# Loading the weights of a two-layer expert network in pairs of pieces: one transfer of 1 MB in place of two of 512 KB

## Chip, cores and metric

One core of one Trainium2 chip. The metric is device time in microseconds (us) of the whole kernel, the median of its runs. In the profile PE is TensorE (matmuls; PEld are its weight loads), DVE VectorE, ACT ScalarE, POOL GpSimd, SP SyncE, whose queue (SPq) issues nearly all transfers here. Lnnn is a line of the kernel.

## The reference, cut to what matters

Chunked attention (4 batches, 8 heads, 768 positions of 64), then a soft mixture of 8 experts with 4 slots each, then a dense layer with a softmax-like activation, layer normalisation and an output matrix:

```python
# attention, per chunk of 32 queries: 8 memory keys + up to 56 keys around it
scores = scale * np.matmul(q_c, k_full.transpose(0, 1, 3, 2))
out[:, :, c_start:c_end] = np.matmul(softmax(scores), v_full)
# experts: x is [3072, 512], phi [512, 32], w1 [8, 512, 1024], w2 [8, 1024, 512]
slot_input = softmax_over_tokens(x @ phi).T @ x
for e in range(E):
    h = np.maximum(slot_input[e] @ w1[e], 0.0)
    slot_out[e] = h @ w2[e]
x = softmax_over_slots(x @ phi) @ slot_out
# dense: w_in [512, 1024], w_out [1024, 512]
h = x @ w_in
solu = h * softmax(h)
return (layer_norm(solu) * g_ln) @ w_out
```

All is float32. The weights w1 and w2 are 33.6 MB, w_in and w_out 4.2 MB, the packed keys, queries and values 25.9 MB.

## The kernel before, in words

**Attention** (lines 841 to 874) runs over 32 groups g, each half a sequence of one pair of heads. Every engine has its order written out by hand. In group g, PE multiplies queries and keys of group g + 1 (`emit_qk`, L254), then the weights and values of group g - 1 (`emit_pv`, L310), and turns blocks round for groups g and g - 3 (L292, L321). SP issues the packed keys and queries of group g + 4 (`load_qk`, 400 KB, L188, into 4 buffers in turn), then `load_e(LOADS[g])`, weight pieces ahead of their use, then the values of group g + 3 in two transfers (`load_v`, L202, 4 buffers; it waits for the `emit_pv` that read the buffer). `emit_spread` (L299 to L303) moves the keys of group g + 3 to the layout that PE reads: those with an odd number on POOL alone, those with an even number on ACT and POOL. PE's product for a group waits for its spread. A few groups carry more work: logits and running sums of the experts' slots, and from group 3 on the casts of w_in to a wider form (`win_ops`; floats on ACT, L577, others on DVE and POOL), which give the raw piece's slot back.

**Weight pieces.** All weights come as 80 pieces of 512 KB, [128 partitions, 1024 floats], rows of 4096 bytes. The list `chunks` fixes their order: w_in and w_out in turn (8 of w_in, 7 of w_out), then the experts' units, two pieces to a unit, then the last piece of w_out. A unit is half of an expert's w1 or w2; there are 32, in the order w1(0,0), w1(0,1), w1(1,0), w2(0,0), w1(1,1), w2(0,1), w1(2,0), and so on to w2(7,0), w2(7,1). `load_e(n)` (lines 219 to 236) issues the next n pieces of the list, and stops at the first that finds no free slot. w_out has slots of its own (w0 to w7). All else takes the first of the list `free`: 4 pieces in e1, 9 in e2, 4 in e3, and the slot w7 that the last piece of w_out needs only at the end. The slots of e3 and w7 are used by expert weights once (`once`). `release` gives a slot back after its last reader. As attention ends, its buffers become slots as well (`more`): 5 in a0 from group 30 on, then 1 in x2, 6 in a1, 1 in x0. A transfer into such a slot waits for the last reader of what lay there.

**Experts** (lines 931 to 951): for each unit n, `emit_w1` (L497) or `emit_w2` (L515), 4 matmul steps, each on half a piece; a turn of w1's result (L504), with work of ACT and DVE between; then `release` of the unit's two pieces and `load_e()`. Steps of the casts of w_out and of the tokens' weights run beside them.

**Dense layer** (from line 953): on PE 24 tiles of 24 matmuls (L723), which with their surroundings take the second half of the kernel. Its weights are in SBUF by then.

The loads in attention are set by one list, and the pieces issued by the end of group g are g - 1 from group 5 on:

```python
LOADS = [0] + [1, 1, 1, 0] + [1] * 28
```

Of the kernel before, what the change touches and what calls it, by code (L numbers as in the profile page):

```python
# [16 lines left out]
P = 128  # L17
# [12 lines left out]
DM = H * D  # L30
KC = DM // P
E, SE, FF = 8, 4, 1024
NSLOT = E * SE
FC = FF // P
# [7 lines left out]
NE = 25  # L42
CAST0, CASTN, NEARLY = 3, 3.4, 8
VLEAD = 3
LOADS = [0] + [1, 1, 1, 0] + [1] * 28
LANE, SIDE = 2.6, 1

CASTU = (0, 1, 2, 3, 4, 5, 6)
# [31 lines left out]
def tile_kernel(ctx: ExitStack, tc: tile.TileContext, kr, vr, w1, w2, w_in, w_out, cst, out):  # L80
    nc = tc.nc
    pe, dve, act, pool, sp = nc.tensor, nc.vector, nc.scalar, nc.gpsimd, nc.sync
# [76 lines left out]
    w_in_f = at("win", 0, KC * FF)  # L159
    w_in_sb = w_in_f.rearrange("p (k f) -> p k f", k=KC)  # L160
    mhi = at("win", 0, FF, FP32R)
    free = [at(n, 1024 * i, 1024) for n, c in (("e1", 4), ("e2", 9), ("e3", NE - 13 - FC)) for i in range(c)]
    wslot = [at(f"w{j}", 0, 1024) for j in range(FC)]
    once = free[13:]
    free.append(wslot[-1])
    whi, wlo = {}, {}

    sint = at("misc", 0, 128).rearrange("p (k s) -> p k s", k=KC)
# [36 lines left out]
    for e in range(E - 1):  # L205
        units += [("w1", e + 1, 0), ("w2", e, 0), ("w1", e + 1, 1), ("w2", e, 1)]
    units += [("w2", E - 1, 0), ("w2", E - 1, 1)]
    chunks = [(w, j) for j in range(2 * KC) for w in ("win", "wout")][:-1]
    for u in units:
        chunks += [u[:2] + (2 * u[2] + j,) for j in range(2)]  # L210
    chunks.append(("wout", FC - 1))
    slot_of = {}
    nxt = [0]

    def more(name, n):

        free.extend(at(name, 1024 * i, 1024) for i in range(n))

    def load_e(n=99):
        while n and nxt[0] < len(chunks):  # L220
            key = chunks[nxt[0]]
            if key[0] == "wout":
                slot = wslot[key[1]]
            elif free:
                slot = free.pop(0)
            else:
                break
            slot_of[key] = slot
            if key[0] in ("w1", "w2"):
                src = (w1 if key[0] == "w1" else w2)[key[1], key[2]]  # L230
                sp.dma_start(out=slot.rearrange("p (k f) -> p k f", k=2), in_=src)
            else:
                src = (w_in if key[0] == "win" else w_out)[key[1]]
                sp.dma_start(out=slot.bitcast(I64), in_=src)
            nxt[0] += 1
            n -= 1

    def release(key):
        if slot_of[key] is wslot[-1]:
            return  # L240
        if key[0] == "win" or not any(slot_of[key] is x for x in once):
            free.append(slot_of[key])


    def kwin(i, c):
# [751 lines left out]
def layout(inputs):  # L997
    import numpy as np

    q, k, v = inputs["q"], inputs["k"], inputs["v"]  # L1000
    mk, mv = inputs["mem_k"], inputs["mem_v"]
    f = np.float32
    a = {}
    qv = q.reshape(B, PAIRS, 2, 2, GTOK, D).transpose(0, 3, 1, 2, 5, 4)
    fill = mk[:, :, 0:1, :]
    kp = np.concatenate([np.repeat(fill, 16, 2), k, np.repeat(fill, NREC * CH - S - 16, 2)], 2)
    kp = np.stack([np.concatenate([kp[:, :, CH * i:CH * (i + GREC) - NMEM], mk], 2) for i in (0, GCH)], 1)
    kp = kp.reshape(B, 2, PAIRS, 2, KT, D).transpose(0, 1, 2, 3, 5, 4)
    a["kr"] = np.concatenate([kp, qv], -1).reshape(GROUPS, P, KT + GTOK)
    vp = np.zeros((B, H, NREC * CH, VW), f)  # L1010
    vp[:, :, 16:16 + S, 0:D] = v
    vp[:, :, 16:16 + S, D] = 1.0
    vp = vp.reshape(B, H, NREC, CH, VW)
    mp = np.ones((B, H, NCH, NMEM, VW), f)
    mp[..., 0:D] = mv[:, :, None]
    vp = np.concatenate([vp[:, :, 0:NCH], mp, vp[:, :, 1:NREC, 0:WIN - REC]], 3)
    vp = vp.reshape(B, PAIRS, 2, 2, GCH, WIN, VW).transpose(0, 3, 1, 2, 5, 4, 6)
    a["vr"] = np.ascontiguousarray(vp).reshape(GROUPS, 2, WIN, VS)
    a["w1"] = np.ascontiguousarray(
        inputs["moe_w1"].reshape(E, 2, 2, P, 2, 512).transpose(0, 4, 1, 3, 2, 5).reshape(E, 4, P, 2, 512)  # L1020
    )
    a["w2"] = np.ascontiguousarray(inputs["moe_w2"].reshape(E, 4, 2, P, DM).transpose(0, 1, 3, 2, 4))
    a["w_in"] = np.ascontiguousarray(
        inputs["moe2_w_in"].reshape(DM, FC, 4, 32).transpose(0, 2, 1, 3).reshape(KC, P, 2, 512).transpose(0, 2, 1, 3).reshape(2 * KC, P, 512)
    ).view(np.int64)
# [33 lines left out]
```

## Time and profile before

| | us |
|---|---|
| three runs, median (lowest to highest) | 333.23 (332.99 to 333.95) |
| the profiled execution, its own time | 334.36 |
| its span, first to last instruction | 332.5 |
| PE busy in the span | 300.8 (90%) |
| DVE, ACT, POOL busy | 239.4, 223.1, 169.9 |
| moved by the DMA engines | 95.86 MB |

The span is cut into 40 equal slices of 8.3 us; a digit is the busy share in tenths, GB/s what the 16 DMA engines moved. An issue's duration is the time that SP's queue is occupied with it; its landing is counted from the start of the issue. A wait is put down to what ended it.

### The profile page before, as it was taken

The numbers are of one execution on the slowest core, as the hardware profiler recorded it, in microseconds if no ns is written. First come the engines' busy times: TensorE is split into PE (matmuls) and PEld (weight loads), VectorE is DVE, ScalarE is ACT, GpSimd is POOL, SyncE is SP. The second block draws the span as 40 slices with busy tenths as digits, with TensorE's granted clock in tenths as the row PEclk, the third lists the DMA queues.
The fourth block names the chain that finished last, engine by engine and source line by source line (L and its number), as shares of the span: only waits on it lengthen the run. The fifth ranks groups of instructions, "written<-read, shape, count | busy, mean of one in ns | idle before, by whom it ended". The sixth has DMA issues, their size and how long they took to land.

```text
span 332.5 us, 8398 instructions
## 1 busy us (share of the span) xinstructions
PE 300.8 (90%) x3069; PEld 218.1 (66%) x3069; DVE 239.4 (72%) x432; ACT 223.1 (67%) x441; POOL 169.9 (51%) x398
## 2 busy tenths in 40 slices
PE   2979698897897789888999999999999999999996
PEld 2667576675675533332434788888888888888885
DVE  6686887797768438999117886897888778787540
ACT  3476656764765427685524779998888888888721
POOL 5436567566767023222100357777767677676600
PEclk9999999999999999999999999999999999999999
DMA  7999999999999999999950004667666756666531
GB/s 286 366 359 405 407 399 411 412 411 414 409 407 396 418 417 419 415 421 416 417 228 0 0 34 158 252 206 264 207 244 211 246 209 201 240 231 234 202 95 64
DMA packets 39433, 95.86 MB, mean 288 GB/s; under 512 B 4832, under 2 KB 15456, under 8 KB 39392
## 3 DMA queue, kind: packets, MB, share of 16 engines
q1 hardware_dynamic: 39248, 95.11, 75.3%
q8 instruction: 24, 0.39, 0.5%
q10 hardware_dynamic: 144, 0.22, 0.2%
q14 instruction: 17, 0.14, 0.1%
HBM read 78.53 MB, written 16.78 MB: 287 GB/s over the span
## 4 chain that ended last, share of the span: by engine, by line
PE 56%; DMA 32%; DVE 5%; ACT 2%; issue 2%; POOL 1%; SPq 1%; ACTq 0%; POOLq 0%
PE bank L723 37%; DMA kq_area<-in_kr_dram 19%; DMA ex_area<-in_w_dram 6%; DMA e_area<-in_w_dram 6%; PE h L635 4%; PE bank L254 3%; PE bank L310 2%; PE bank L497 1%; POOL kq_area L303 1%; PE bank L292 1%; DMA vz_area<-in_vr_dram 1%; PE bank L515 1%; PE bank L733 1%; PE t L733 1%; PE t L692 1%
## 5 line engine op out<-in xcount | busy, mean ns | idle before, releaser
L723 PE MATMUL bank<-wh_area,yh_area 128*128 128x512 f32 x552 | 129.8, 390 | 0.0
L723 PEld LDWEIGHTS bank<-wh_area,yh_area 128*128 128x128 f32 x552 | 103.4, 188 | 21.8
L303 POOL TENSOR_SCALAR kq_area<-kq_area 64x416 f32<-64x416 f32 x88 | 38.5, 443 | 38.5 <-DMA kq_area<-in_kr_dram 27.9
L254 PE MATMUL bank<-kq_area 128*32 128x128 f32 x768 | 29.8, 293 | 16.8 <-POOL kq_area L303 10.8
L706 DVE STREAM_TRANSPOSE yq_area<-yq_area 128x1024 f32<-128x1024 f32 x20 | 24.9, 1246 | 17.2 <-DMA yq_area<-z 17.2
L254 PEld LDWEIGHTS bank<-kq_area 128*32 128x32 f32 x768 | 21.0, 116 | 23.1 <-POOL kq_area L303 15.2
L650 DVE SCALAR_TENSOR_TENSOR eb_area<-h,eb_area 128x1024 f32<-128x1024 f32 x24 | 29.0, 1213 | 9.2 <-ACT eb_area L644 9.0
L295 ACT COPY s_area<-bank 128x384 f32<-128x384 f32 x32 | 15.2, 476 | 27.7 <-PE bank L292 26.1
L310 PE MATMUL bank<-vz_area,s_area 128*32 128x130 f32 x768 | 29.7, 279 | 2.2 <-ACT s_area L295 1.6
L272 DVE TENSOR_REDUCE cst_area<-bank 128x6 f32<-128x384 f32 x32 | 17.7, 554 | 19.2 <-PE bank L254 19.0
L688 POOL TENSOR_SCALAR cst_area<-cst_area 128x1 f32<-128x1 f32 x72 | 26.6, 369 | 7.6
L641 DVE TENSOR_REDUCE cst_area<-h 128x1 f32<-128x1024 f32 x24 | 29.0, 1216 | 0.9 <-PE h L635 0.9
L644 ACT ACTIVATE eb_area<-h,cst_area 128x1024 f32<-128x1024 f32 x24 | 26.6, 1110 | 1.9 <-DVE cst_area L641 1.9
L673 ACT ACTIVATE eb_area<-eb_area,cst_area 128x1024 f32<-128x1024 f32 x24 | 27.3, 1138 | 0.1
L677 POOL TENSOR_SCALAR cst_area<-cst_area 128x1 f32<-128x1 f32 x24 | 15.9, 662 | 21.7 <-ACT eb_area L644 19.8
L717 DVE TENSOR_TENSOR yh_area<-yq_area,yh_area 128x1024 fp32r<-128x1024 f32 x20 | 24.5, 1224 | 2.3 <-ACT yh_area L713 2.3
L670 ACT ACTIVATE eb_area<-eb_area,cst_area 128x1024 f32<-128x1024 f32 x20 | 23.1, 1155 | 4.3 <-DVE eb_area L650 3.8
L310 PEld LDWEIGHTS bank<-vz_area,s_area 128*32 128x32 f32 x768 | 22.3, 111 | 5.0 <-ACT s_area L295 2.8
L689 POOL TENSOR_SCALAR cst_area<-cst_area 128x1 f32<-128x1 f32 x72 | 21.9, 304 | 7.1
L713 ACT CAST yh_area<-yq_area 128x1024 fp32r<-128x1024 f32 x20 | 21.0, 1049 | 6.3 <-DVE yq_area L706 6.3
L741 ACT ACTIVATE eb_area<-bank,cst_area 128x512 f32<-128x512 f32 x23 | 15.8, 685 | 8.8 <-POOL cst_area L679 5.9
L299 ACT COPY kq_area<-kq_area 64x416 f32<-64x416 f32 (+1 forms) x34 | 12.2, 407 | 11.2 <-DMA kq_area<-in_kr_dram 11.1
(154 smaller groups left out, 534.2 us busy)
## 6 DMA issues: line engine op xcount, KB each, us to landing
e_area<-in_w_dram SPq DMA_DIRECT2D x37, 512.0 KB, 8.5
ex_area<-in_w_dram SPq DMA_DIRECT2D x26, 512.0 KB, 10.0
kq_area<-in_kr_dram SPq DMA_DIRECT2D x32, 400.0 KB, 6.3
vz_area<-in_vr_dram SPq DMA_DIRECT2D x64, 195.0 KB, 6.3
z<-eb_area SPq DMA_DIRECT2D x20, 512.0 KB, 2.7
yq_area<-z SPq DMA_DIRECT2D x80, 128.0 KB, 2.9
out_dram<-eb_area SPq DMA_DIRECT2D x23, 256.0 KB, 2.1
e_area<-in_w_in_dram SPq DMA_DIRECT2D x8, 512.0 KB, 6.4
```

The lines of the kernel that those rows point to most:

```text
L254: pe.matmul(out=bk[32 * j:32 * j + 32, t * 128:(t + 1) * 128], lhsT=kq[i][:, KT + c * CH:KT + (c + 1) * CH], rhs=kwin(g % 2, c), start=Tru ...
L303: pool.tensor_scalar(out=o, in0=i, scalar1=1.0, scalar2=0.0, op0=ALU.mult, op1=ALU.add)
L310: pe.matmul(out=bk[32 * j:32 * j + 32, t * 2 * VW:(t + 1) * 2 * VW], lhsT=atb[g % 2][:, c * CH:(c + 1) * CH], rhs=vz[g % 4][:, :, c * VW:( ...
L641: dve.tensor_reduce(out=sc("nm", i), in_=fin["h"][i % 2], axis=AX.X, op=ALU.max, negate=True)
L644: act.activation(out=eb[i % FIN], in_=fin["h"][i % 2], func=ACTF.Exp, bias=sc("nm", i), accum_out=sc("s", i))
L650: dve.scalar_tensor_tensor(out=ub[i % FIN], in0=fin["h"][i % 2], scalar=-1.0 / FF, in1=eb[i % FIN], op0=ALU.mult, op1=ALU.mult, accum_out= ...
L670: act.activation(out=yb[i % FIN], in_=ub[i % FIN], func=ACTF.Identity, scale=-float(FF), bias=sc("nu", i))
L673: act.activation(out=sq, in_=ub[i % FIN], func=ACTF.Square, scale=-float(FF), bias=sc("nu", i), accum_out=sc("vs", i))
L688: pool.tensor_scalar(out=t, in0=r, scalar1=r, scalar2=xx, op0=ALU.mult, op1=ALU.mult)
L706: dve.transpose(out=yv[i % FIN].rearrange("p (f a t) -> p a f t", f=FC, a=4), in_=yq[i % FIN].rearrange("p (a f t) -> p a f t", f=FC, a=4),)
L717: dve.tensor_tensor(out=yl[i % FIN][:, sl], in0=tps(i, sl) if i < NPE else yv[i % FIN], in1=yh[i % FIN][:, sl].bitcast(FP32), op=ALU.subtract,
L723: pe.matmul(out=fin["o"][i % 2], lhsT=a[i % FIN][:, f * 128:(f + 1) * 128], rhs=w[f], start=start, stop=stop)
```

## The change

The two pieces of a unit, and pieces 2j and 2j + 1 of w_in, become one transfer of 1 MB with rows of 8192 bytes into a pair of neighbouring slots. Pieces of w_out, the first unit and the last two units stay single. Slots are split in two lists: `free` has the pairs (2 in e1, 4 in e2, 2 in e3, later 2 in a0 and 3 in a1), `ones` the odd pieces (the ninth of e2, w7, later one each in a0, x2, x0). A pair is given back when both its pieces are. The order of the list becomes: a pair of w_in, two single pieces of w_out, and so on; then the units as before. A call of `load_e` counts pieces and may go one over. The list LOADS now has two pieces in every second group; the host lays the weights out so that a pair's row is contiguous. The code that reads the weights is the same.

```diff
-LOADS = [0] + [1, 1, 1, 0] + [1] * 28
+LOADS = [0, 2, 0, 2, 0] + [0, 2] * 14
...
-    free = [at(n, 1024 * i, 1024) for n, c in (("e1", 4), ("e2", 9), ("e3", NE - 13 - FC)) for i in range(c)]
+    free = [at(n, 2048 * i, 2048) for n, c in (("e1", 2), ("e2", 4), ("e3", (NE - 13 - FC) // 2)) for i in range(c)]
     wslot = [at(f"w{j}", 0, 1024) for j in range(FC)]
-    once = free[13:]
-    free.append(wslot[-1])
+    once = free[6:]
+    ones = [at("e2", 8 * 1024, 1024), wslot[-1]]
...
+    def halves(u):
+        return [u[:2] + (2 * u[2] + j,) for j in range(2)]
+
+    chunks = []
+    for j in range(0, 2 * KC, 2):
+        chunks.append([("win", j), ("win", j + 1)])
+        chunks += [[("wout", i)] for i in (j, j + 1) if i < FC - 1]
+    for n, u in enumerate(units):
+        chunks += [[x] for x in halves(u)] if n == 0 or n >= len(units) - 2 else [halves(u)]
+    chunks.append([("wout", FC - 1)])
...
-        free.extend(at(name, 1024 * i, 1024) for i in range(n))
+        free.extend(at(name, 2048 * i, 2048) for i in range(n // 2))
+        if n % 2:
+            ones.append(at(name, 1024 * (n - 1), 1024))
...
-        while n and nxt[0] < len(chunks):
-            key = chunks[nxt[0]]
+        while n > 0 and nxt[0] < len(chunks):
+            keys = chunks[nxt[0]]
+            kind, two = keys[0][0], len(keys) == 2
...
+            elif free if two else ones:
+                slot = (free if two else ones).pop(0)
             else:
                 break
...
-            n -= 1
+            n -= len(keys)
...
     def release(key):
-        if slot_of[key] is wslot[-1]:
+        slot, keys, two, kind = pair_of[key]
+        gone.add(key)
+        if not all(k in gone for k in keys) or slot is wslot[-1]:
             return
-        if key[0] == "win" or not any(slot_of[key] is x for x in once):
-            free.append(slot_of[key])
+        if kind == "win" or not any(slot is x for x in once):
+            (free if two else ones).append(slot)
...
-        inputs["moe_w1"].reshape(E, 2, 2, P, 2, 512).transpose(0, 4, 1, 3, 2, 5).reshape(E, 4, P, 2, 512)
+        inputs["moe_w1"].reshape(E, 4, P, 2, 512).transpose(0, 3, 2, 1, 4)
```

## Rows read from the trace of the kernel before

**Rows 1.** The page: the DMA engines in 40 slices of 8.3 us.

```profile
DMA  7999999999999999999950004667666756666531
GB/s 286 366 359 405 407 399 411 412 411 414 409 407 396 418 417 419 415 421 416 417 228 0 0 34 158 252 206 264 207 244 211 246 209 201 240 231 234 202 95 64
```

**Rows 2.** Stretches: us, busy of PE, PEld, DVE, ACT, POOL, clock, DMA share, GB/s.

```profile
14.00:21.00 7.00, 7.00 (x174) 5.68 (x165) 5.35 (x15) 4.89 (x13) 2.40 (x6) 1.00 0.93 307
60.00:95.00 35.00, 30.68 (x669) 23.98 (x669) 27.84 (x73) 24.28 (x68) 21.30 (x39) 1.00 1.03 411
124.00:136.00 12.00, 11.64 (x95) 4.41 (x91) 10.06 (x24) 9.09 (x21) 3.40 (x4) 1.00 1.03 420
```

**Rows 3.** Timeline of SP's queue, 9 to 15 us, and of ACT at 20.

```profile
9.63 0.43 SPq L234 DMA_DIRECT2D e_area<-in_w_in_dram  x1
12.88 1.12 SPq L202 DMA_DIRECT2D vz_area<-in_vr_dram  x2
...
14.67 0.94 SPq L234 DMA_DIRECT2D w_area<-in_w_out_dram  x1
...
19.98 0.69 ACT L577 ACTIVATE cst_area<-e_area 128x512 f32<-128x512 f32 x1
```

**Rows 4.** The last keys: issue and landing (min/median/max), then POOL's and PE's timeline.

```profile
L188 SPq DMA_DIRECT2D kq_area<-in_kr_dram x1: 333/333/333, 94.9 to 94.9; - x1
...
DMA to landing us min/median/max: 6.3/6.3/6.3
...
101.36 2.12 POOL L303 TENSOR_SCALAR kq_area<-kq_area 64x416 f32<-64x416 f32 x4 [0.23 <-DMA kq_area<-in_kr_dram]
...
103.54 0.86 PE L254 MATMUL bank<-kq_area 128*32 128x128 f32 x24 [1.37 <-POOL kq_area L303]
```

**Rows 5.** DMA queues: packets, MB, share of 16 engines; 128.5 to 131.5, 38.0 to 38.4 us.

```profile
q1 hardware_dynamic: 344, 1.26, 102.4%
...
q14 instruction: 1, 0.01, 4.8%
```

**Rows 6.** Timeline of SP's queue around the first units, from 119 us.

```profile
119.87 0.33 SPq L231 DMA_DIRECT2D ex_area<-in_w_dram  x1
123.40 7.78 SPq L231 DMA_DIRECT2D e_area<-in_w_dram  x8
...
124.30 0.38 SPq L231 DMA_DIRECT2D e_area<-in_w_dram  x1
...
129.91 0.33 SPq L231 DMA_DIRECT2D e_area<-in_w_dram  x1
```

**Rows 7.** The 43rd piece of weights: issue, and time to landing.

```profile
L231 SPq DMA_DIRECT2D ex_area<-in_w_dram x1: 328/328/328, 116.1 to 116.1; - x1
...
DMA to landing us min/median/max: 10.1/10.1/10.1
```

**Rows 8.** Timeline of PE: the first two units of the experts, and the last two.

```profile
122.31 1.92 PE L497 MATMUL bank<-e_area,cst_area 128*32 128x512 f32 x16 [0.27 <-DVE cst_area L426]
...
168.04 1.97 PE L515 MATMUL bank<-e_area,hr_area 128*32 128x512 f32 x8
170.24 2.21 PE L515 MATMUL bank<-e_area,hr_area 128*32 128x512 f32 x8 [0.24 <-DMA e_area<-in_w_dram]
```

**Rows 9.** The chain that ended last, 125 to 175 us: start, us, what.

```profile
161.61 9.74 DMA e_area<-in_w_dram
...
171.40 1.05 PE bank L515 x4
```

**Rows 10.** Issues by line, KB each, median us to landing; last, the keys' min/median/max.

```profile
z<-eb_area SPq DMA_DIRECT2D x20, 512.0 KB, 2.7
yq_area<-z SPq DMA_DIRECT2D x80, 128.0 KB, 2.9
e_area<-in_w_in_dram SPq DMA_DIRECT2D x8, 512.0 KB, 6.4
...
DMA to landing us min/median/max: 4.0/6.3/7.3
```

More of the change, by code (lines that the diff above doesn't have):

```diff
@@ L207, in tile_kernel @@
     units += [("w2", E - 1, 0), ("w2", E - 1, 1)]
[L208 to L212, printed above, removed]
+    def halves(u):
[4 more added lines that the diff above has]
+        chunks += [[("wout", i)] for i in (j, j + 1) if i < FC - 1]
@@ L213, in tile_kernel @@
+    for n, u in enumerate(units):
+        chunks += [[x] for x in halves(u)] if n == 0 or n >= len(units) - 2 else [halves(u)]
+    chunks.append([("wout", FC - 1)])
+    slot_of, pair_of = {}, {}
     nxt = [0]
     def more(name, n):
-        free.extend(at(name, 1024 * i, 1024) for i in range(n))
+        free.extend(at(name, 2048 * i, 2048) for i in range(n // 2))
+        if n % 2:
+            ones.append(at(name, 1024 * (n - 1), 1024))
     def load_e(n=99):
-        while n and nxt[0] < len(chunks):
-            key = chunks[nxt[0]]
[L222 to L225, printed above, removed]
+        while n > 0 and nxt[0] < len(chunks):
+            keys = chunks[nxt[0]]
+            kind, two = keys[0][0], len(keys) == 2
+            if kind == "wout":
+                slot = wslot[keys[0][1]]
+            elif free if two else ones:
+                slot = (free if two else ones).pop(0)
@@ L226, in load_e @@
             else:
                 break
[L228 to L231, printed above, removed]
+            for i, key in enumerate(keys):
+                slot_of[key] = slot[:, 1024 * i:1024 * i + 1024]
+                pair_of[key] = (slot, list(keys), two, kind)
+            if kind in ("w1", "w2"):
+                src = (w1 if kind == "w1" else w2)[keys[0][1], keys[0][2] // 2]
+                if not two:
+                    half = keys[0][2] % 2
+                    src = src[:, 2 * half:2 * half + 2]
+                sp.dma_start(out=slot.rearrange("p (k f) -> p k f", f=512), in_=src)
@@ L232, in load_e @@
             else:
-                src = (w_in if key[0] == "win" else w_out)[key[1]]
+                src = w_in[keys[0][1] // 2] if kind == "win" else w_out[keys[0][1]]
                 sp.dma_start(out=slot.bitcast(I64), in_=src)
             nxt[0] += 1
-            n -= 1
+            n -= len(keys)
+    gone = set()
     def release(key):
-        if slot_of[key] is wslot[-1]:
+        slot, keys, two, kind = pair_of[key]
+        gone.add(key)
+        if not all(k in gone for k in keys) or slot is wslot[-1]:
@@ L1019, in layout @@
     a["w1"] = np.ascontiguousarray(
-        inputs["moe_w1"].reshape(E, 2, 2, P, 2, 512).transpose(0, 4, 1, 3, 2, 5).reshape(E, 4, P, 2, 512)
+        inputs["moe_w1"].reshape(E, 4, P, 2, 512).transpose(0, 3, 2, 1, 4)
     )
-    a["w2"] = np.ascontiguousarray(inputs["moe_w2"].reshape(E, 4, 2, P, DM).transpose(0, 1, 3, 2, 4))
+    a["w2"] = np.ascontiguousarray(inputs["moe_w2"].reshape(E, 2, 4, P, DM).transpose(0, 1, 3, 2, 4))
     a["w_in"] = np.ascontiguousarray(
-        inputs["moe2_w_in"].reshape(DM, FC, 4, 32).transpose(0, 2, 1, 3).reshape(KC, P, 2, 512).transpose(0, 2, 1, 3).reshape(2 * KC, P, 512)
+        inputs["moe2_w_in"].reshape(DM, FC, 4, 32).transpose(0, 2, 1, 3).reshape(KC, P, 1024)
     ).view(np.int64)
```

## The prediction

> **What bounds the kernel now.** I read the slices of the page first. The DMA engines are busy to the full from the second slice to the twentieth, that is from 8 to 166 us, at 359 to 421 GB/s, and then stop [rows 1]. The weights, the queries, keys and values all pass in that time, so the first half of the kernel is a stream of bytes. The stages say the same with more detail: from 60 to 95 us the stream runs at 411 GB/s with PE at 30.7 of 35 us, from 124 to 136 us at 420 GB/s; only from 14 to 21 us is there a shortfall, 307 GB/s at a busy share of 0.93, while PE is full [rows 2]. At its other end, the last weight piece of 512 KB is issued at 161.61 us, lands 9.74 us later, and 1.05 us of matmuls behind it end the expert stage at 172.45 [rows 9]. Those 9.74 us are 7.8 pieces at 420 GB/s (1.25 us each): SP keeps eight transfers in the air, in order. What follows 172.45 is fixed work on PE with weights that are already there. So the question is when that last piece lands, and when PE could be done without it.
>
> PE's side of it: its last two units stretch to 1.97 and 2.21 us, where the first two took 1.92 together [rows 8]. Without the DMA they would end at about 168.04 + 1.92 = 170.0 us, 2.4 us before the real end. More than that a faster stream cannot give, unless the expert stage starts earlier.
>
> **The change part by part.**
>
> *Fewer, longer transfers.* 4 pairs of w_in and 29 of the 32 units' pairs become one transfer each: 33 issues less, at 0.33 us of SP [rows 6]. SP waits in this stage, for landings and free slots, so this alone is worth nothing. The bytes are the same. A row of 4096 bytes costs 102.4% of 16 x 3.0 us over 1.26 MB, 307 rows of 4096 bytes (the other 37 packets only tell of an end), or 160 ns; a packet of 8192 bytes that stands alone in its queue, one of instructions, takes 4.8% of 16 x 0.4 us, 307 ns [rows 5]. Two rows against one: 13 ns at most, call it 11 without the end packets; over the 8 rows that each of the 16 engines has of a pair that is 0.09 us a pair, 2.9 us for 33. Nothing at all is the other end, if the packet starts that it saves lie under their neighbours (the share is over 100%). I take the middle, 0.044 us a pair, b = 1.45 us in all, because that packet belongs to another kind of transfer.
>
> The Trainium skill ("DMA: Bandwidth & Descriptors", Where 436 GB/s comes from) puts the ports' limit at 435 GB/s; by it 34.6 MB would gain at most 2.9 us over 420 GB/s (an estimate), and the sum below would be 0.3 us where it is 1.35.
>
> *The early order.* In group 1 the kernel now queues two pieces instead of one (issue at 9.63 us), and none in group 2 (14.67) [rows 3]; groups 3 and 4 have two and none. SP then stands until 12.88 for PE, and behind this comes the shortfall: 2.15 MB in 7.0 us would take 5.23 us at 411 GB/s, so 1.77 us are lost [rows 2]. A piece more in the queue is 1.25 us of work just ahead of the hole. I take a = 1.25 us gained; bounds 0 (if the shortfall only moves) and 1.8 (all of it). Nothing new is waited for there: such a piece lands 6.4 us after its issue [rows 10], the pair then at about 9.63 + 6.4 + 1.25 = 17.3, and the first cast runs on ACT at 19.98 [rows 3].
>
> *The order of weights against keys.* Counting the pieces that load_e has issued through group 26: 25 before (LOADS is 1 a group from group 5 on), 27 after, since group 18 takes a half and a whole pair, three pieces for its 2. The last keys, kq(31), are issued at 94.90 in group 27 behind these, and land 6.3 us later at 101.2; POOL spreads them from 101.36, and PE, idle for 1.37 us, starts on them at 103.54 [rows 4]. They are what the end of the attention waits for. Two pieces more ahead of them cost 2.5 us; of these the early order takes off 1.25, and the 9 pairs that are through by then 0.40. PE's expert stage starts x = 0.85 us later: 122.31 [rows 8] becomes 123.16. By itself this is covered, for the stage then has 2.4 us to spare against the DMA; with that cover gone it costs 0.85.
>
> *Slots.* The region arithmetic decides the rest. Before, 46 pieces fit ahead of the first unit's matmuls; after, 13 pair slots and 5 single ones hold fewer in order, since three singles (the odd ends of the regions that come free late) can only take the last two units: 43 pieces are issued, and the 44th, half of unit 14's pair, waits until unit 1 gives its pair back (the first unit returns a single, which no pair can use). Before, the SP queue shows the same wait without damage: it issues the 46th piece at 119.87, waits for PE until 123.40, and has 6 us of work in the air. After, this cover is gone. The 43rd piece was issued at 116.1 and landed 10.1 us later, 126.2 [rows 7]; with 1.25 and 17 pairs x 0.044 off that is 124.2. The pair's release came at 124.30 (the issue behind unit 1's wait) [rows 6], after the change at 125.15. So the queue is empty, and a fresh transfer needs its own delay L before bytes arrive. L from rows: a 512 KB store lands in 2.7 us, less 1.25 of bytes, 1.45; a 128 KB fetch in 2.9, less 0.31, 2.6; the first keys of the program in 4.0, less 0.98, 3.0 [rows 10]. I take 2.4, near the fetch, which reads HBM as this does, and on the short side because the core is not cold. The hole is S1 = 125.15 + 2.4 - 124.2 = 3.35 us.
>
> A second one follows. Units 3 and 4 lie in slots that are used once, so unit 16's pair waits for unit 5, whose release let SP issue at 129.91 [rows 6]; that becomes 130.76, and bytes come at 133.16. Units 14 and 15 have landed by 125.15 + 2.4 + 2 x 2.46 = 132.47. S2 = 0.7 us. From unit 6 on a slot comes back with each unit, faster than the 2.46 us that a pair needs, and the stream holds.
>
> **The sum.** The last piece lands at 171.35 - 1.25 (a) - 1.45 (b) + 3.35 + 0.7 = 172.7. PE, from 170.0 + 0.85 = 170.85, is ready before, so the DMA still sets the end, 1.35 us later than now. Written out with the unknowns left in: 1.3 + L - a - 0.75 b (what delays or hurries the keys moves the dry moment and the release alike). The profiled execution took 334.36 us, 332.5 of it span, and is 1.13 above the median of the three runs; I put the 1.35 on that median: 333.23 + 1.35 = 334.6 us.
>
> **The rivals.**
>
> *The stream never runs dry, and the change is a gain.* If the transfers in the air still cover 125 to 128 us, S1 and S2 are nothing, the last piece lands at 168.7, and PE sets the end at 170.85, 1.6 us before the present one: 331.6 us. It decides at one point, whether unit 14's pair is issued at least L before unit 13's has landed. For it: before, there were 6.5 us in hand there (119.87 + 10.1 against 123.40) [rows 6, 7], and my count takes 3 pieces, 3.75 us, and 2.5 us from these. Against it: that leaves nothing for L, whose smallest row is 1.45. A page's rule leads the same way: the Trainium skill ("DMA: Bandwidth & Descriptors", Rules for kernel authors) wants at least 1 MiB per transfer for full bandwidth. The trace differs on pieces of 512 KB, which already run at 420 GB/s [rows 2] with eight in the air. 0.15.
>
> *It cancels.* a and b near their upper ends and L near its lowest: 1.3 + 1.45 - 1.8 - 0.75 x 2.0 = -0.5; with L at 1.8, about -0.2. Taken as no change, 333.2 us. 0.27.
>
> *Rows of 8192 bytes are cut.* If the queue makes two packets of 4096 of each, b is 0 and the sum is 1.3 + 2.4 - 1.25 = 2.5: 335.7 us. Only the packet size of another queue speaks against it [rows 5]. The Trainium skill ("DMA: Bandwidth & Descriptors", SWDGE vs HWDGE vs iDMA) prefers packets of at most 4096 bytes, which would be this case; no weight row before is longer, so no run here shows it. 0.08.
>
> *The attention limps.* Keys with an odd number now come 4.4 us behind the even ones instead of 3.2, the even ones 2.0 behind these. Two groups take 6.4 us of stream and 2 x 3.2 x 30.7 / 35 = 5.6 of PE [rows 2], so the waits ought to merge; if 0.2 us were lost in each of 13 rounds, unit 1's release would come 2.6 us later still, the hole would grow by it, and the time be 337.2. 0.05.
>
> **How the numbers follow.** 0.45 is left for the forecast, 334.6, with its own range of 333.6 to 336.5. A measurement of this kernel can tell 0.3%, 1.0 us, from no change. Of the forecast's 0.45 a part of 0.10 falls below 334.2 and counts as the same. Slower: 0.35 + 0.08 + 0.05 = 0.48; same: 0.27 + 0.10 = 0.37; faster: 0.15. The range takes in the cancelling case and the gain, which is its lower end, and above it L at 3.0 with nothing of a: 1.3 + 3.0 - 1.1 = 3.2, 336.5.
>
> **What would show it.** In the slices the GB/s should dip once, in the slice or two between 124 and 133 us, and 14 to 21 us should fill up. SP's wait in line with the release of unit 1 should end at about 125, with the landing of unit 13's pair ahead of it, and the transfer behind it should land within 5 us instead of 16 or more. The last keys should land at about 102, the last piece near 172.7, with PE waiting for it. 8192-byte rows should show as half the packets. I am wrong if the stream stays full through 124 to 133 us (the slots were miscounted), if the keys land earlier than 101 (the order costs nothing), or if the last piece lands before 171 with the hole in place (a longer row saves more than I allow).

## The result, and the profile after the change

| | us |
|---|---|
| before, median of 6 runs (lowest to highest) | 333.68 (332.99 to 334.63) |
| after, median of 6 runs | 337.55 (336.34 to 341.1) |
| ratio, 95% interval | 1.0126 [1.0076, 1.0175] |
| after, the profiled execution and its span | 336.34, 334.5 |
| forecast, its range | 334.6, 331.6 to 336.5 |

The change makes the kernel slower, as forecast, but by 3.9 us where 1.4 was said, and outside the range. The profiled execution is the fastest of the six, so what it shows is the mildest case. A ratio leaves out the runs more than 1.5% above the fastest of the same kernel, which the medians and spans beside it take in: two in all, 341.49 us in *No triple load* and 336.55 us in the second run of *Both edits*.

First the page of after, DMA engines in 40 slices (against [rows 1]), and its packets on the main queue.

```profile
DMA  7999999999999979999960004656666665766521
GB/s 291 388 407 387 411 412 415 412 419 413 408 415 399 402 288 361 421 428 423 413 272 0 1 33 157 240 207 251 228 238 206 231 222 179 264 222 236 208 89 64
...
q1 hardware_dynamic: 34496, 95.11, 73.8%
```

The early slices are fuller than before, and there is one dip that was not there, slices 15 and 16, from 117 to 134 us. Before, the same queue had 39248 packets for the same 95.11 MB: 4752 less, which is 33 transfers x 128 rows and 16 end packets for each. So rows of 8192 bytes go as one packet.

The stretches of [rows 2], after (us, busy of PE, PEld, DVE, ACT, POOL, clock, DMA share, GB/s):

```profile
14.00:21.00 7.00, 5.65 (x118) 4.24 (x122) 4.71 (x13) 3.42 (x10) 2.40 (x6) 1.00 1.02 403
60.00:95.00 35.00, 27.44 (x629) 21.97 (x622) 24.91 (x66) 22.14 (x64) 21.45 (x38) 1.00 1.03 413
124.00:136.00 12.00, 11.65 (x99) 4.46 (x99) 10.14 (x24) 9.09 (x21) 3.48 (x4) 1.00 0.90 337
```

The shortfall of 14 to 21 us is filled, 403 GB/s for 307; but PE, full there before, now works 5.65 of the 7 us, and 27.44 of the 35 from 60 us, where it had 30.68. The hole is in the last row, 337 GB/s for 420.

The hole from near by: the timeline of SP's queue from 112 to 134 us, what SP waited for there, then the two transfers at its edge, unit 13's pair (issue, time to landing) and unit 14's.

```profile
112.12 1.28 SPq L245 DMA_DIRECT2D ex_area<-in_w_dram  x3
124.24 9.25 SPq L245 DMA_DIRECT2D e_area<-in_w_dram  x6
...
SPq L245 <- PE bank L515: 12.9, 4, 10.8
...
L245 SPq DMA_DIRECT2D ex_area<-in_w_dram x1: 432/432/432, 113.0 to 113.0; - x1
...
DMA to landing us min/median/max: 11.6/11.6/11.6
...
L245 SPq DMA_DIRECT2D e_area<-in_w_dram x1: 327/327/327, 124.2 to 124.2; - x1
...
DMA to landing us min/median/max: 4.7/4.7/4.7
```

SP has three pairs out by 113.4 us and then stands 10.8 us for PE, until unit 1 gives its pair back at 124.24. Unit 13's pair lands at 113.0 + 11.6 = 124.6, so the queue is empty as the next one is issued. That one lands 4.7 us later, at 128.91, and so 4.31 us behind its forerunner, where a pair in a full stream needs 2.45: 1.9 us more. It does not end there. By the trace the next pairs land at 132.07, 134.54, 137.70, 140.76 and 143.20: three of these steps take 3.1 us instead of 2.45, 2.0 us more.

The bytes tell where the loss lies. First one line of before, then four of after:

```profile
112.00:124.00 12.00, 9.91 (x85) 4.92 (x80) 4.29 (x15) 3.75 (x15) 2.14 (x2) 1.00 1.03 418
```

```profile
112.00:124.00 12.00, 9.91 (x84) 4.91 (x80) 4.29 (x15) 3.78 (x16) 2.15 (x2) 1.00 0.88 358
124.00:128.90 4.90, 4.90 (x44) 1.99 (x44) 3.18 (x9) 4.56 (x11) 0.51 (x1) 1.00 0.75 244
128.90:132.00 3.10, 3.10 (x28) 0.97 (x24) 3.00 (x8) 1.63 (x5) 1.72 (x2) 1.00 0.99 373
132.00:143.00 11.00, 9.58 (x79) 3.28 (x71) 10.56 (x23) 7.75 (x19) 2.13 (x3) 1.00 1.01 422
```

Against 418 GB/s, 1.7 us are missing already before 124, while the last pairs of the queue land, 2.0 to 128.9 and 0.4 to 132: 4.1 us in all. From 132 us on the stream is full, so the late landings at 137.70 and 140.76 are no new holes; they show at the landings what was lost before.

The last keys (issue, landing, POOL's spread, PE's product, against [rows 4]), PE's longest wait in the attention, its first unit, and the end of the chain:

```profile
L188 SPq DMA_DIRECT2D kq_area<-in_kr_dram x1: 535/535/535, 94.5 to 94.5; - x1
...
DMA to landing us min/median/max: 7.1/7.1/7.1
...
101.74 1.88 POOL L321 TENSOR_SCALAR kq_area<-kq_area 64x416 f32<-64x416 f32 x4 [0.54 <-PE bank L328]
...
103.67 0.86 PE L272 MATMUL bank<-kq_area 128*32 128x128 f32 x24 [1.30 <-POOL kq_area L321]
...
77.62 0.86 PE L272 MATMUL bank<-kq_area 128*32 128x128 f32 x24 [3.33 <-POOL kq_area L321]
...
122.25 0.62 PE L515 MATMUL bank<-e_area,cst_area 128*32 128x512 f32 x2 [0.27 <-DVE cst_area L444]
...
158.10 15.20 DMA e_area<-in_w_dram
173.30 0.04 issue
173.35 1.05 PE bank L533 x4
```

The last keys land at 101.6, and the experts begin at 122.25, as early as before. The last piece lands at 173.30, 1.94 us later than in the profile of before, and the time is 1.98 longer: half of the 3.9 us between the medians. The other half is that after's profile lies 1.2 us below its median and before's 0.7 above. The wait of 3.33 us before 77.62 is new: before, PE's longest wait for keys behind the first was 1.82 us. It stands ahead of group 23, whose keys are issued behind the three pieces of group 18.

One identity holds through all that follows. In each of the 17 profiled executions, before and after included, the time less the landing of the last expert piece is 162.9 to 163.15 us. So that landing sets the end, whatever the kernel, and every experiment can be read by it.

A slip of the description ahead: w_in and w_out are stored as float64 (4.2 MB each) and cast to float32 on the chip; no step rests on it.

### The profile page after: what moved, and what is told of

Same layout as the page of the kernel before. It is cut to its first block, busy times and chain, and to the rows that moved or that the text cites. A ratio compares the mean times of both kernels' runs of the same rounds, so it can differ in the third digit from the quotient of the medians.

```text
span 334.5 us, 8330 instructions
## 1 busy us (share of the span) xinstructions
PE 297.9 (89%) x3069; PEld 216.4 (65%) x3069; DVE 236.6 (71%) x432; ACT 222.8 (67%) x441; POOL 170.7 (51%) x398
## 3 DMA queue, kind: packets, MB, share of 16 engines
q1 hardware_dynamic: 34496, 95.11, 73.8%
## 4 chain that ended last, share of the span: by engine, by line
PE 54%; DMA 28%; DVE 10%; ACT 3%; POOL 2%; issue 2%; SPq 0%; ACTq 0%; DVEq 0%; POOLq 0%
PE bank L741 36%; DMA e_area<-in_w_dram 9%; DMA kq_area<-in_kr_dram 7%; DMA w_area<-in_w_out_dram 6%; DMA e_area<-in_w_in_dram 5%; PE h L653 4%; PE bank L272 2%; POOL kq_area L321 2%; PE bank L328 2%; DMA vz_area<-in_vr_dram 1%; PE bank L515 1%; PE bank L351 1%; PE bank L398 1%; PE bank L310 1%; PE bank L751 1%
## 5 line engine op out<-in xcount | busy, mean ns | idle before, releaser
L706 POOL TENSOR_SCALAR cst_area<-cst_area 128x1 f32<-128x1 f32 x72 | 26.8, 372 | 7.6
L328 PE MATMUL bank<-vz_area,s_area 128*32 128x130 f32 x768 | 27.5, 273 | 1.0 <-ACT s_area L313 1.0
L695 POOL TENSOR_SCALAR cst_area<-cst_area 128x1 f32<-128x1 f32 x24 | 15.7, 656 | 23.7 <-ACT eb_area L662 21.8
L691 ACT ACTIVATE eb_area<-eb_area,cst_area 128x1024 f32<-128x1024 f32 x24 | 27.3, 1139 | 0.1
L707 POOL TENSOR_SCALAR cst_area<-cst_area 128x1 f32<-128x1 f32 x72 | 23.4, 324 | 7.1
L328 PEld LDWEIGHTS bank<-vz_area,s_area 128*32 128x32 f32 x768 | 21.4, 108 | 2.2 <-ACT s_area L313 1.9
L305 ACT ACTIVATE s_area<-s_area 128x384 f32<-128x384 f32 x32 | 16.9, 529 | 3.7 <-DVE s_area L296 3.7
```

Source lines behind the costliest of these rows:

```text
L328: pe.matmul(out=bk[32 * j:32 * j + 32, t * 2 * VW:(t + 1) * 2 * VW], lhsT=atb[g % 2][:, c * CH:(c + 1) * CH], rhs=vz[g % 4][:, :, c * VW:( ...
L691: act.activation(out=sq, in_=ub[i % FIN], func=ACTF.Square, scale=-float(FF), bias=sc("nu", i), accum_out=sc("vs", i))
L706: pool.tensor_scalar(out=t, in0=r, scalar1=r, scalar2=xx, op0=ALU.mult, op1=ALU.mult)
L707: pool.tensor_scalar(out=r, in0=t, scalar1=1.5, scalar2=r, op0=ALU.add, op1=ALU.mult)
```

## The experiments

Each was timed in five rounds beside the kernel before, whose medians in the four sets were 333.83, 333.16, 333.08 and 332.94 us. "Clock" is the mean granted clock of a run.

**The changed kernel, again.** No edit.

> The changed kernel once more, for its spread and its granted clock. Slots theory (the DMA queue runs dry between 124 and 131 us, all else is as before): every run within 0.3% of 336.3 us, clock 1.00 in each, 2.0 to 2.6 us over the kernel before. Clock theory (the gap of 3.3 us that PE now has at 74 us, where three pieces of weights stand ahead of one group's keys, lets TensorE's clock fall in some runs, on top of the slots): clock of 0.985 to 0.995 in about half of the runs, those 0.5 to 5 us over the ones at 1.00, and in a profile of such a run a stretch at half clock that begins in or just after that gap.

338.44 us (336.9 to 340.22, 6 runs), ratio 1.0151 [1.0112, 1.0191]. The loss is there again. All six runs had a clock of 0.985 to 0.995; before, 78 of 104 runs of the four sets had 0.998 or more. The stretch in question, 70 to 78 and 78 to 82 us, and PE's product for group 23:

```profile
70.00:78.00 8.00, 4.07 (x100) 3.26 (x92) 4.23 (x13) 5.33 (x15) 3.92 (x8) 1.00 1.02 414
78.00:82.00 4.00, 4.00 (x65) 3.28 (x60) 2.71 (x7) 1.37 (x6) 1.70 (x3) 0.57 1.04 418
...
77.58 0.93 PE L272 MATMUL bank<-kq_area 128*32 128x128 f32 x24 [3.93 <-POOL kq_area L321]
```

PE stands 3.93 us for the keys, and behind that the granted clock is 0.57 on average from 78 to 82 us, the lower of its two levels (1.2 GHz) nearly throughout. Nothing like it is in the attention of the profile before. The kernels below show the same: without the hole, half clock from 81.9 to 85.3 behind a wait of 3.46 us; with rows of 4096 bytes, from 78.7 to 82.1 behind one of 2.88. Of the twelve waits of 2 us and more that PE has after the first keys, in all the profiles together, seven have such a stretch and five do not, after's own 3.33 us among them. Three more stretches before 130 us stand behind shorter waits (1.81 us, and twice 0.8 at most).

**The hole closed.** Units 14 and 15 as single pieces, which take the three odd slots, so that 46 pieces are out ahead of unit 1 as before.

```diff
-  if n == 0 or n >= len(units) - 2
+  if n in (0, 14, 15) or n >= len(units) - 2
```

> Units 14 and 15 as single pieces too: they take the four odd slots that no pair can use, so 46 pieces are issued ahead of the first unit's end, as before the change, instead of 43. Slots theory: no stretch below 415 GB/s between 122 and 135 us, the last weight piece lands 3.5 to 4 us earlier than 173.3, near 169.5, and PE, not the DMA, sets the end of the expert stage near 170 to 171: 331.5 to 332.5 us in runs at full clock. Clock theory: the same gain, but still runs at 0.985 to 0.995 and a spread of several us, since the gap at 74 us is left. If the long transfers themselves are slow (rival), the dip stays at 299 GB/s and the time stays at 336 or more.

334.42 us (332.53 to 337.3, 12 runs), ratio 1.0029 [0.9999, 1.0059]. The stretch of the hole, and SP's queue there:

```profile
124.00:136.00 12.00, 11.72 (x97) 4.53 (x97) 7.22 (x18) 7.74 (x17) 4.50 (x4) 1.00 1.02 423
...
115.34 4.00 SPq L245 DMA_DIRECT2D ex_area<-in_w_dram  x6
126.57 2.80 SPq L245 DMA_DIRECT2D e_area<-in_w_dram  x3
```

SP still waits for PE until 126.57, but with pieces in the air that last to 132.4, and the stream runs at 423 GB/s. Against the changed kernel 3.2 to 4.1 us are back (1.0126 or 1.0151 less 1.0029, of 333 us). The hole is the main loss. The time is not the 331.5 to 332.5 us that was expected from the slots alone, and all twelve runs have a clock of 0.995 or less. In its profile (335.8 us, above its median) the last piece lands at 172.93 for all the closed hole: from 21 to 60 us the stream moved 388 GB/s there, where before had 406, with half clock from 27.3 to 30.7. So the attention can lose in the stream what the hole gives back.

**No triple load.** One piece instead of two behind group 18, so that no group's keys stand behind three.

```diff
-LOADS = [0, 2, 0, 2, 0] + [0, 2] * 14
+LOADS = [0, 2, 0, 2, 0] + [0, 2] * 6 + [0, 1] + [0, 2] * 7
```

> LOADS[18] is 1 instead of 2, so that group 18 issues one piece and not three, and 25 pieces stand ahead of the last keys instead of 27. Clock theory: the longest gap of PE in the attention falls from 3.3 to about 2.2 us, every run is at clock 0.999 or more, and the spread shrinks to 0.3% around 335 to 336.3 us. Slots theory alone: the last keys land 2 to 2.5 us earlier (99 to 99.6), the expert stage starts up to 2 us earlier, the release of unit 1 with it, and the hole shrinks by as much: 334.3 to 335 us, with no change of the spread.

338.22 us (333.9 to 341.49, 6 runs), ratio 1.0102 [1.0053, 1.0151]. The hole stays, and the gain is 0.8 to 1.6 us by the ratios, within the intervals; by the medians there is none. Both theories of the expectation missed: five of six runs have a clock of 0.995 or less, and the time is far above 334.3 to 335 us. Its profile (338.59) shows why it can be as slow as after: unit 14's pair is issued 2 us later than after's, and the end comes 2.25 us later. Half clock stood from 37.5 to 40.9 us, behind a wait of 2.75, and from 122.8 to 126.3, on the experts' first units. First PE's unit 1 in after; then the same unit in this kernel, the stretch, and the issue of unit 14's pair:

```profile
123.14 1.04 PE L515 MATMUL bank<-e_area,cst_area 128*32 128x512 f32 x8
```

```profile
124.23 1.96 PE L515 MATMUL bank<-e_area,cst_area 128*32 128x512 f32 x8
...
122.80:126.20 3.40, 3.40 (x17) 0.54 (x13) 0.00 (x0) 1.62 (x3) 1.51 (x1) 0.51 0.21 87
...
L245 SPq DMA_DIRECT2D e_area<-in_w_dram x1: 327/327/327, 126.2 to 126.2; - x1
```

PE begins its first unit at 122.66 us here and at 122.25 in after, but gives unit 1's pair back at 126.23 and 124.24: 1.6 of the 2 us are the half clock on two units' matmuls, while the queue is empty and the stream waits for them.

**Both edits.** The hole closed and no triple load.

> Units 14 and 15 single, and one piece instead of two behind group 18, so that no group has three pieces ahead of its keys. Theory (gaps and clock): the gap of 3.5 us ahead of group 23 goes, others of 1.5 to 2.7 us stay, so the clock still falls in many runs; between 333.4 and 334.2 us, no more than 1 us below the run with the single units alone (334.42). Rival (the triple load is all that is left of the loss): 333.2 us or below, clock 1.0 in most runs.

332.13 us (331.1 to 335.22, 12 runs), ratio 0.9983 [0.9957, 1.0009]. Then once more, in another set:

> The same kernel as in the run with both parts, once more. Theory (hole and triple load are all that turned the change into a loss, early order and long rows together are worth some 1 us): 332.1 us, 0.2 to 0.3 per cent below the kernel before. Rival (no gain is left): level with it, 333.1 us.

331.87 us (330.77 to 336.55, 12 runs), ratio 0.9963 [0.9946, 0.9981]. In this set it is faster than the kernel before, by 1.2 us, where the first run's interval touches no change; than the changed one it is faster by 5 to 6. Its stretches of [rows 2] with 140 to 160 us, and its last landing:

```profile
14.00:21.00 7.00, 5.30 (x120) 4.00 (x116) 4.17 (x13) 3.49 (x9) 2.41 (x6) 1.00 1.00 400
60.00:95.00 35.00, 31.01 (x665) 23.85 (x658) 27.36 (x71) 23.22 (x66) 23.17 (x43) 1.00 1.03 407
124.00:136.00 12.00, 11.37 (x91) 4.36 (x91) 11.07 (x25) 9.11 (x22) 3.58 (x4) 1.00 1.02 426
140.00:160.00 20.00, 17.29 (x144) 6.22 (x138) 17.25 (x36) 14.02 (x33) 6.30 (x7) 1.00 1.01 427
...
153.51 15.15 DMA e_area<-in_w_dram
```

PE is back to 31.01 of 35 us from 60 us, and the last piece lands at 168.66, 2.7 us ahead of the profile of before (which is itself about 1 us slower than the medians of before). With e1 and e2 this makes a table of two by two, ratios to before:

| | three pieces behind group 18 | two at most |
|---|---|---|
| hole | 1.0126, 1.0151 | 1.0102 |
| no hole | 1.0029 | 0.9983, 0.9963 |

Down a column the hole costs 3.2 to 4.6 us; along a row the triple load costs 0.8 to 1.6 with the hole and 1.5 to 2.2 without. The second is clear of noise in one of the two runs only (0.9946 to 0.9981 against 0.9999 to 1.0059).

**The order alone.** Single pieces and slots as before, with the order of the list and LOADS of after.

```diff
-    chunks = [(w, j) for j in range(2 * KC) for w in ("win", "wout")][:-1]
+    chunks = []
+    for j in range(0, 2 * KC, 2):
+        chunks += [("win", j), ("win", j + 1)] + [("wout", i) for i in (j, j + 1) if i < FC - 1]
```

> The kernel before, with its single pieces of 512 KB and all its slots, but with the order of the pieces and the LOADS of the changed kernel. There is no triple load and no loss of slots. If the early order fills the shortfall of 14 to 21 us (1.25 to 1.8 us) and nothing else happens: the last piece lands near 169.8, PE sets the end, and the time is 1 to 1.6 us below the kernel before, 332 to 332.6 us, clock 1.00. If the order itself costs time (uneven groups in the attention, or a falling clock): the same or slower, 333.7 or more, with clocks under 0.999.

333.23 us (332.46 to 335.0, 12 runs), ratio 0.9993 [0.9971, 1.0014]: no difference, where 1 to 1.6 us less was expected of the filled shortfall. Its profile fills 14 to 21 us (411 GB/s), but from 21 to 60 us the stream runs at 398 GB/s, 406 before. It has uneven groups but no triple load, and 10 of its 12 runs are at a clock of 0.995 or less. The one seems to take what the other gives, but no run here parts them.

**The length of the rows.** As with the hole closed, with transfers of 1 MB but two rows of 4096 bytes for each of 8192.

```diff
+  sp.dma_start(out=slot.rearrange("p (t f) -> p t f", t=2),
+               in_=w[keys[0][1], c:c + 2].rearrange("t p k f -> p t (k f)"))
```

> As e1_singles, one transfer of 1 MB to a pair at the same places of the queue, but laid out in HBM as two pieces, so that its rows are 4096 bytes long again. If rows of 8192 bytes are what saves (forecast: 0.044 us a pair, 1.3 us over the 31 pairs): pairs land 2.46 us apart or more where those of e1_singles land 2.42 to 2.48, and the time is 0.5 to 1.3 us over e1_singles. If a longer row saves nothing: the same time within 0.5 us and the same spacing.

334.79 us (333.46 to 336.36, 11 runs), ratio 1.005 [1.0029, 1.007], against 1.0029 with long rows: 0.7 us, within the intervals. The stream tells more. From 140 to 160 us, long rows, then short ones, then the kernel before:

```profile
140.00:160.00 20.00, 16.20 (x132) 5.99 (x132) 19.43 (x40) 12.83 (x32) 5.57 (x6) 1.00 1.01 427
```

```profile
140.00:160.00 20.00, 16.48 (x131) 5.86 (x124) 19.29 (x42) 12.84 (x30) 5.56 (x6) 1.00 1.02 418
```

```profile
140.00:160.00 20.00, 16.51 (x132) 5.90 (x131) 18.54 (x39) 13.99 (x33) 5.29 (x6) 1.00 1.03 418
```

The other profiles agree: in this stretch the 13 with long rows move 423 to 427 GB/s, the four with short rows 418. A pair of 1.049 MB takes 2.456 us at 427 and 2.509 at 418: 0.053 us a pair, and it is the row, not the size of the transfer, that gives it.

**Long rows alone, the early order alone, and the two together.** The kernel before, with 16 pairs as one transfer each after the attention wherever two neighbouring slots are free (long rows); with two pieces in group 1 and none in group 2 (early order); with both.

```diff
+                two = n > 50 and half == 0 and key[:2] + (key[2] // 2,) not in units[-2:] and free
+                two = two and place[id(free[0])] == (place[id(slot)][0], place[id(slot)][1] + 1)
...
+                    sp.dma_start(out=whole.rearrange("p (k f) -> p k f", k=4), in_=src)
```

```diff
-LOADS = [0] + [1, 1, 1, 0] + [1] * 28
+LOADS = [0] + [2, 0, 1, 0] + [1] * 28
```

> The kernel before in its order, its LOADS and its slots; only from the end of the attention on, where both pieces of a unit find neighbouring free slots, they go as one transfer of 1 MB with rows of 8192 bytes (16 pairs). No hole, no uneven groups. If long transfers save 0.044 us a pair: 0.7 us at the landing of the last piece, 333.0 us against 333.7, at full clock. If they save nothing: the same as before within 0.3 us. If they cost (rival: a pair can only be read when it has landed whole): 334 or more.

> The kernel before with one change: two pieces in group 1 and none in group 2, and from group 3 on the LOADS as they were, so that no later group is uneven. If a piece more ahead of the shortfall of 14 to 21 us is worth its 1.25 us: GB/s of 400 instead of 307 in that stretch, the last keys land 1.0 to 1.3 us earlier, the last weight piece lands near 170.2, and the time is 1.0 to 1.3 us below the kernel before. If the shortfall only moves, or PE's own pace decides there: within 0.3 us of it.

> e6_pairs_fit and e7_early together: what of the change can be had without the uneven groups and without the loss of slots. If both theories of the gain hold: 1.7 to 2.0 us below the kernel before, where PE begins to set the end of the expert stage. If the gain of the early order is real and that of the rows is not: as e7_early.

> The kernel before with the early order in even groups and 16 pairs as transfers of 1 MB behind the attention, once more, since its interval touched no change. Theory (a and b are real but small where nothing is traded for them): 332.8 us, 0.1 to 0.2 per cent below the kernel before, full clock in most runs. Rival (no gain at all): 333.3 us, level with it.

Long rows alone: 333.64 us, ratio 1.0008 [0.9986, 1.0031]. Early order alone: 333.13, 0.9988 [0.9967, 1.0008]. Both: 332.82, 0.9986 [0.9966, 1.0006]; once more, 333.05, 0.9996 [0.9978, 1.0014]. None can be told from no change; the point estimates are +0.3, -0.4 and -0.3 us. The early order fills its stretch here too, and PE pays for it: the stretch, and PE's product of keys at its end.

```profile
14.00:21.00 7.00, 4.95 (x120) 3.98 (x124) 4.28 (x13) 3.52 (x9) 2.41 (x6) 1.00 1.03 410
...
20.70 0.54 PE L254 MATMUL bank<-kq_area 128*32 128x128 f32 x12 [2.05 <-POOL kq_area L303]
```

PE was busy for all 7 us before and is for 4.95 now, since the piece that fills the hole stands ahead of the keys. From 21 to 60 us the stream then runs at 397 GB/s, 406 before, with half clock from 22.2 to 25.6.

**Filling PE's waits.** Does the fallen clock cost the time, or do the late keys? Dummy matmuls, whose result nothing reads, ahead of the keys' product of the groups where PE waited longest: 34 in the changed kernel and in the one with the hole closed.

```diff
+  for _ in range(FILL.get(g + 1, 0)):
+      pe.matmul(out=bank(2)[:, 384:512], lhsT=ident, rhs=ident, start=True, stop=True)
   emit_qk(g + 1)
```

> The changed kernel with 33 dummy matmuls of 128x128 (an estimate of 0.32 us each, a third of the 0.97 us that one dummy of 128x384 takes before the experts) ahead of the keys' matmuls of the odd groups, where PE stood longest: 9 of them (some 2.9 us) ahead of group 23, where the gaps of 3.3 to 3.9 us were, 1 to 5 elsewhere. They write columns that nothing reads. Theory (the long gaps of PE cost the granted clock, and that costs time in most runs): no stretch at half clock in the attention, most runs at a clock of 0.998 or more, and a median near 336.4 us, the one run of the changed kernel at full clock, instead of 338; the hole of the stream stays, with its 4 us. Rival (the lower clock is of the chip and not of the gaps, or it is harmless): clocks of 0.985 to 0.995 as before and a median near 338, or full clock and 338 all the same.

> The same dummy matmuls in the kernel without the hole (units 14 and 15 single). Theory: 334.4 us was the gain of a full stream less 1 us and more for the clock; at full clock 333.2 us or a little below, level with the kernel before, and with the filled kernel above it the hole shows alone: 3 to 4 us between the two. Rival (the clock is not the gaps' doing): 334.4 us at clocks of 0.983 to 0.995.

339.44 us (338.26 to 339.7, 4 runs), 1.0185 [1.0168, 1.0203], and 335.5 (333.33 to 336.54, 7 runs), 1.0062 [1.0038, 1.0086]. The clock stood at 1.0 in three of the four runs of the first, but neither became faster. The dummies (34, not the 33 of the expectation) had a wait of their own:

```profile
L863 PE MATMUL bank<-cst_area x68: 275/275/377, 21.9 to 104.6; 128*128 128x128 f32 x68
...
  ACT s_area L314: 11.7, 20
```

They write the bank that ACT still copies from, so PE stood for ACT, and unit 1's release came at 125.94 instead of 124.24. This test says nothing on the clock's price. Its mend: 26 dummies in the bank of the keys' product itself, and 20 in the kernel with both edits.

```diff
-      pe.matmul(out=bank(2)[:, 384:512], ...
+      pe.matmul(out=bank((g + 1) % 2)[:, 384:512], ...
```

> The changed kernel with 26 dummy matmuls (0.31 us each by the run before, 8.1 us in all) ahead of the keys' matmuls of the nine groups before which PE stood longest; they now write a bank that the keys' matmuls behind them wait for anyway, and take up about two thirds of each gap. Theory (the fallen clock is a part of the loss): clock 0.998 or more in most runs, and a median of 336.3 us, 1.5 below the changed kernel. Rival (the late keys are the loss, the clock only tells of them): full clock and 337.6 to 338.4 us all the same, since the keys come no earlier.

> The kernel without the hole and without three pieces ahead of one group's keys (332.13 us, five of 12 runs at a clock of 0.995 or less), with 20 such dummies in its seven longest gaps. Theory: all runs near full clock, the runs at 334.6 to 335.2 us go, median 331.5. Rival (the dummies hold PE up, or the slow runs come from elsewhere): 332.1 us or more, with runs of 334 to 335 still there.

The changed kernel: 336.94 us (336.37 to 337.69, 4 runs), 1.0118 [1.0093, 1.0143], with three of four runs at 0.998 or more. That is 0.6 and 1.5 us below the two medians of the changed kernel, and no run is above 338, but the intervals overlap. The kernel with both edits: 332.68 us (331.24 to 335.25, 12 runs), 0.9981 [0.9953, 1.0008]: no gain from the dummies. The stretches 70 to 78 and 78 to 90 us of the first:

```profile
70.00:78.00 8.00, 6.49 (x136) 5.72 (x132) 4.19 (x14) 5.85 (x17) 4.27 (x8) 1.00 1.02 415
78.00:90.00 12.00, 11.00 (x236) 8.62 (x228) 10.17 (x28) 7.40 (x22) 7.19 (x14) 1.00 1.03 415
```

PE works on through the wait and the clock stays at 1.00. So filling the waits keeps the clock, and by the medians the changed kernel gets 0.6 to 1.5 us back with it; that the clock itself was the price is not shown by these two, since the kernel with both edits got nothing. The runs of before add that its 26 below 0.998 were slower than the other 78, by 0.4 to 0.7 us in the mean of each of the four sets; whether the clock is the cause there or only comes with it, they do not tell.

## Why the prediction was wrong

*The hole was right in place and cause, and in size for the profile shown, there partly by luck.* The slots ran out at the 44th piece; unit 13's pair landed at 124.60 (said 124.2), SP's wait ended at 124.24 (said 125.15), and 4.1 us of bytes are missing (said 3.35 + 0.7 = 4.05). The delay L of a fresh transfer was 4.67 - 2.46 = 2.2 us (said 2.4). The release came 0.9 us earlier than said, since PE began its units at 122.25 (said 123.16); but what follows the release took longer. The last piece lands 49.06 us behind it in after and 49.1 to 49.3 in the other four profiles with the hole, where the sum has 172.7 - 125.15 = 47.55. The term that is too small there is the second hole: 0.7 us was said, and 2.0 us are lost at the landings behind the first. In those four profiles the stream moves 334 to 343 GB/s from 112 to 136 us, 419 before, which is 4.4 to 4.9 us of bytes. Closing the hole gives back 3.2 to 4.6 us.

*The keys were right, the price of PE's waits was not.* The last keys landed at 101.6 (said about 102). But "the waits ought to merge" failed. Three pieces ahead of group 23's keys make PE stand for 3.3 to 3.9 us, and other waits of 1 to 2.8 us stand where the pairs are. In the changed kernel what PE loses by them counts in full. The profiled executions with the hole, issue of unit 14's pair (unit 1's release) and own time:

| | release | time | difference |
|---|---|---|---|
| after | 124.24 | 336.34 | 212.10 |
| after with fewer fillers | 124.48 | 336.71 | 212.23 |
| after, again | 124.74 | 336.90 | 212.16 |
| after with 34 fillers | 125.94 | 338.26 | 212.32 |
| no triple load | 126.23 | 338.59 | 212.36 |

With the queue empty, the rest of the kernel hangs on this release: every 1 us that PE loses in the attention is 1 us of the time. Without the hole the same difference runs from 207.7 (the hole closed, with fillers) to 209.9 us (both edits, with fillers), for the stream does not wait there. By this table after's median, 337.55, stands for a release near 125.3 (an estimate), which is about what was said, 125.15. But the prediction set its 1.35 us on the median of before, 333.23, and not on the profile from which its rows came, 334.36: it let PE run 1.13 us earlier, as in the best case. Its own landing of 172.7 would be 335.7 us. So of the 2.95 us between 334.6 and 337.55 some 1.1 are this step, 1.6 what follows the release, and 0.2 the release itself.

The prediction gave this rival ("the attention limps", 337.2 us, 0.05) nearly its right time, by luck: the cause is not 0.2 us in each round, but a few long waits and the half clock. The triple load, which the prediction counted, is the longest wait and costs 0.8 to 2.2 us by the ratios.

*a and b are there as bytes, hardly as time.* In after's profile the early order fills the shortfall (403 GB/s for 307, 0.67 MB or 1.6 us of stream; said 1.25, bound 1.8), and a long row saves 0.053 us a pair (said 0.044). As time they were worth 2.7 us in the sum (1.25 + 1.45); alone or together in the kernel before they give 0.5 us or less, and with hole and triple load taken out of the change some 1 us (0.9983 and 0.9963, mean 0.9973, of 333). Where a goes, the profiles show. Of the 15 with the early order five reach only 357 to 367 GB/s from 14 to 21 us, the other ten 396 to 413; and from 21 to 60 us ten of the 15 run at 384 to 401 GB/s, 406 before, which loses 0.5 to 2.1 us again. So in most profiles the shortfall in part only moves, the case that the prediction put at a = 0; in after's own profile (406 GB/s there) it did not. What moves it is not settled: PE waits more in 14 to 21 us (busy 5.65 us for 7.0), and half clock stands behind such a wait in some of these profiles, not in all. Why late bytes saved at 140 to 160 us do not all show as time is not settled either.

So the sum: -1 us for all that was meant to gain (said -2.7), the hole 4 (said 4.05, with 0.85 for later keys in it), late keys and clock 1 to 2 (said nothing beyond that 0.85), which is 4 to 5 us for a measured 3.9 to 5.0. The steps that failed are the bet that PE's waits merge, which set the sum on PE's best case; the second hole, 0.7 us for 2.0; and a and b as time, 2.7 us of which some 1 shows.

*The rivals.* "The stream never runs dry" gave 331.6 us; the kernel with the hole closed takes 334.4, and with no triple load besides 331.9 to 332.1. "Rows are cut" is excluded by the packets: 8192 bytes go as one, and rows of 8192 ran at 427 GB/s, rows of 4096 at 418. The Trainium skill ("DMA: Bandwidth & Descriptors", SWDGE vs HWDGE vs iDMA) prefers packets of at most 4096 bytes in a table on the descriptors that GpSimd builds; these transfers are issued by SP, and here the longer packets are the faster ones. The Trainium skill's wish for transfers of at least 1 MiB ("DMA: Bandwidth & Descriptors", Rules for kernel authors) is not borne out here: with several transfers in the air, those of 1 MB with short rows run at 418 GB/s, as 512 KB pieces do.

*The clock* was in no step. That it falls behind long waits of PE is shown in several profiles, though not for every wait. That it can cost time of its own is shown in one: 1.6 us, in the profile of *No triple load*, where it fell on the two units for which the empty queue waited. How much of after's median it makes is not shown; the medians with and without fillers lie 0.6 to 1.5 us apart.

## What to carry to other kernels

When loads are merged, count in the new unit what is in flight at each point where a slot must come back: a slot list that held 46 pieces held 43 as pairs, and that alone turned a gain of 1 us into a loss of over 3. Once a queue has run dry, the release that restarts it is on the path, and every stall upstream of it, harmless before, is paid in full; so price the two together. A transfer moved into a gap of a queue stands ahead of something: look at who waits for that before the gap is counted as gained.

## What the runs showed of the hardware

With the queue run dry, 1 MB needed 4.6 to 4.7 us from issue to landing in four of the five profiles with the hole and 6.0 in the fifth, where pairs of a full stream land 2.45 us apart; behind it single steps of 2.9 to 3.9 us followed, some of them with the stream full again by its bytes (422 GB/s from 132 to 143 us in after). Rows of 8192 bytes moved 423 to 427 GB/s; rows of 4096 moved 418, in transfers of 512 KB as of 1 MB. Behind waits of PE of 2 to 4 us, with PE otherwise working, the granted clock fell to its lower level in seven of twelve cases (0.57 on average from 78 to 82 us behind a wait of 3.93); in the others it stayed at full speed. Eight matmuls that took 1.04 us at full clock took 1.96 at the lower level.
